# Attention of 896 tokens ahead of a two-layer MoE pair, with each narrowed weight used for two chunks of tokens

## The chip, the cores and the metric

One core of one Trainium2 chip runs the whole program as a single launch. The metric is the device time in microseconds (us). TensorE (PE) multiplies, VectorE (DVE), ScalarE (ACT) and GpSimd (POOL) do elementwise work, and SyncE (SP) issues the DMA transfers.

## What is computed

The reference is a chain of three stages over 2304 tokens (4 batches of 576) with a model width of 512:

```python
scores = scale * q @ k.T + bias            # 8 heads of 64; window of 128 keys, causal
attn = softmax(scores);  x = attn @ v      # -> x: 2304 x 512
h = x @ w_in;  g = relu(h) ** 2            # first MoE, d_ff 2048
x = g @ w_out
P = sinkhorn(softmax(x @ w_gate))          # second MoE: 8 experts of 1024
out = sum_e P[:, e] * (relu(x @ w1[e]) @ w2[e])
```

The weights w_in and w_out arrive as 64-bit floats. The kernel makes 32-bit values out of them by bit operations ("narrowing") and splits each into a high and a low part, so that a product is three matmuls.

## The kernel before, in words

**Chunks.** The first MoE walks over five chunks of tokens (lines 50 to 53), 384, 512, 512, 512 and 384 wide, which the text calls chunk zero to chunk four. In each chunk 16 turns f (loop at line 683) take one slice of 128 hidden units: `gemm1` (line 122) makes the product into the bank h1 with 12 matmuls, lines 695 to 698 apply relu (ACT) and the square (DVE), `split_sb` splits the result into gh and gl (ACT, POOL), and, two turns later (LAG), `moe1_tail` (line 488) adds 12 matmuls into four accumulator banks. After the last turn `moe1_finish` takes the accumulators out and `gate_sums` (line 515) runs eight small matmuls into lt; these mark the end of a chunk in the trace.

**Weights.** In chunk zero `moe1_load` (line 473) calls `fetch` (line 458) for the 64-bit slice (tile u, three buffers, 512 KB), `narrow` (line 434), which is three ACT and five DVE instructions, and stores the result to DRAM (d_in for w_in, d_out for w_out, 512 KB each). Tile a (from w_in) has three buffers and b (from w_out) four. In later chunks a and b are loaded back from DRAM. The loads run one or two turns ahead.

**Attention.** The work is cut into 32 units (line 368): a batch, a pair of heads, and either its first 384 tokens ("early", tiles i = 0, 1, 2) or the rest ("rest", tiles 3 and 4). `attention_load` (line 187) fetches q, k and v of a unit, `attention_qk` (line 205) transposes and splits q and k, `attention_scores` (line 257) handles one tile's scores up to the normalised weights, `attention_weights` (line 302) transposes them and splits them into p, and `attention_values` (line 350) multiplies by v and writes the split result into the x of a chunk. `plan` (line 375) writes these steps into one list by hand; in its first run the score step goes two tiles ahead of the weight step and two units alternate, in its second one tile ahead.

**Order.** Before each chunk's turns, line 675 calls `advance` (line 407) to run the list up to what that chunk needs (`needed`, line 401). So four units (384 tokens) come before chunk zero. `part` (line 652), called three times a turn, then hands out the units of the next chunk evenly over the 16 turns: beside chunk zero run the 8 units (20 tiles) for chunk one, beside chunk one the 20 tiles for chunk two, and so on. Units of the first four (`alone`, line 190) rotate their PSUM tiles through more banks: those of the accumulators and of h1 too (`at_ps`, line 162). All instructions up to line 718 are put in order by the framework's scheduler, which starts from the order of the program text; each engine then works through its own list in order, SP's list of DMA issues too.

**Behind it.** From chunk two on nothing differs in the change; the second MoE (two thirds of the time) follows. The lines named in rows: L440 to L454 narrowing, L466/L471 fetches of weights, L481 stores of narrowed weights, L483 loads of a and b, L118 to L120 matmuls of products, L696/L698 relu and square, L109/L110 the split, L282 scores, L322 transposes of the weights, L336 values, L113/L114 splits out of PSUM.

Of the kernel before, what the change touches and what calls it, by code (L numbers as in the profile page):

```python
# [8 lines left out]
F32 = mybir.dt.float32  # L9
F32R = mybir.dt.float32r  # L10
U32 = mybir.dt.uint32
AF = mybir.ActivationFunctionType
# [17 lines left out]
def attention_moe_moe2(  # L30
# [106 lines left out]
    cv = cvs.enter_context(tc.tile_pool(name="cv", bufs=1))  # L137
    att = ExitStack()
    ap = att.enter_context(tc.tile_pool(name="ap", bufs=1, side="right"))

    rel_i = ap.tile([P, 2 * P], mybir.dt.int32, name="rel_i", tag="kl", bufs=2)
    nc.gpsimd.iota(rel_i, pattern=[[-1, 2 * P]], base=P, channel_multiplier=1)
# [41 lines left out]
                    tbias[j * TAIL : (j + 1) * TAIL, hp, :], bias[0:TAIL, 2 * hp + j, : P + TAIL]  # L184
                )

    def attention_load(b, hp, rest):

        h0 = 2 * hp
        t = {"rest": rest, "alone": b == 0 and not rest}  # L190
        for nm, src in (("k", k), ("q", q), ("v", v)):
            r = t[nm] = ap.tile([P, 3, 2, D], F32, name=f"{nm}raw", tag=f"{nm}raw", bufs=2)
            r0 = 0 if not rest else EARLY - (0 if nm == "q" else P)
            r1 = FULL * P if rest else EARLY
            for j in range(2):
                nc.sync.dma_start(
                    r[:, : (r1 - r0) // P, j, :], src[b, h0 + j, r0:r1, :].rearrange("(t p) d -> p t d", p=P)
                )
            if rest:
                nc.sync.dma_start(  # L200
                    r[:TAIL, (r1 - r0) // P], src[b, h0 : h0 + 2, r1:, :].rearrange("j p d -> p j d")
                )
        return t
# [164 lines left out]
    units = [(b, hp, rest) for b in range(B) for rest in (False, True) for hp in range(NPAIR)]  # L368
    ts = {}

    def load(n):
        if n < len(units):
            ts[n] = attention_load(*units[n])

    def plan():


        out = []

        def run(tiles, first, s_ahead, q_ahead):  # L380
            turned = first
            for j, x in enumerate(tiles):
                while turned <= max(n for n, _ in tiles[: j + q_ahead + 1]):
                    out.append(("q", turned, 0))
                    turned += 1
                out.append(("s", *x))
                if j >= s_ahead:
                    out.append(("t", *tiles[j - s_ahead]))
            out.extend(("t", *x) for x in tiles[-s_ahead:])

        run([(n + j, i) for n in range(0, NPAIR, 2) for i in range(3) for j in range(2)], 0, 2, 1)
        run(
            [(n, i) for n in range(NPAIR, len(units)) for i in (range(3, FULL + 1) if units[n][2] else range(3))],
            NPAIR, 1, 1,
        )
        return out

# [2 lines left out]

    def needed(n):

        b, at = divmod(n - 1, S)
        last = (2 * b + (at >= EARLY) + 1) * NPAIR
        return 1 + max(j for j, x in enumerate(steps) if x[0] == "t" and x[1] < last)

    def advance(n):
        for kind, m, i in steps[done[0] : n]:
            b, hp, rest = units[m]
            if kind == "q":  # L410
                if m == NPAIR:
                    tails_ready()
                attention_qk(m, ts[m])
                ts[m]["p"] = {}
            elif kind == "s":
                attention_scores(hp, ts[m], i)
                if i in (1, FULL):
                    attention_v(m, ts[m])
                    load(m + 2)
            else:  # L420
                attention_weights(ts[m], i)
                attention_values(b, hp, ts[m], i)
        done[0] = max(done[0], n)
# [6 lines left out]
    d_in = [dram.tile([P, 2, DM], F32, name=f"d_in{f}") for f in range(NF1)]  # L430
    d_x2 = [dram.tile([P, NK, HALF], F32, name=f"d_x2{h}") for h in range(2 * NB)]
    d_out = [dram.tile([P, 2, DM], F32, name=f"d_out{f}") for f in range(NF1)]

    def narrow(src, hi, lo):

# [37 lines left out]
    def moe1_load(c, f):  # L473
        out = []
        for j, (nm, dr, nb) in enumerate((("a", d_in[f], 3), ("b", d_out[f], 4))):
            hl = mp.tile([P, 2, DM], F32R, name=nm, tag=nm, bufs=nb)
            if c == 0:
                i = 2 * f + j
                fetch(i + 2)
                narrow(words.pop(i), hl[:, 0], hl[:, 1])  # L480
                nc.sync.dma_start(dr, raw(hl))  # L481
            else:
                nc.sync.dma_start(raw(hl), dr)  # L483
            hl = [hl[:, 0], hl[:, 1]]
            out.append([x.rearrange("p (k f) -> p k f", k=NK) if nm == "a" else x for x in hl])
        return out

    def moe1_tail(c, f, accs, g, b):
        c0, n = chunk(c)
# [177 lines left out]
    for c in range(NCH):  # L667
        c0, n = chunk(c)
        if c == 1:
            cvs.close()  # L670
            xp2 = m1.enter_context(tc.tile_pool(name="xp2", bufs=1))
            for i in range(3, NCH):
                new_x(xp2, i)

        advance(needed(c0 + n))
        if c == NCH - 1:
            att.close()
            p2 = ctx.enter_context(tc.tile_pool(name="p2", bufs=1, side="right"))
            p3s = ExitStack()
            p3 = p3s.enter_context(tc.tile_pool(name="p3a", bufs=1, side="right"))  # L680
            load_q(0)
            for nm, eng in (("b11", 0), ("b21", 1), ("t1", 0), ("t2", 1), ("t3", 0), ("t4", 1), ("b22", 0)):
                x_op(nm, (nc.vector, nc.gpsimd)[eng])
        for f in range(NF1):
            now[:] = c, f
            a, bw = ahead.pop(0)
            todo = c * NF1 + f + (2 if loaded[0] < NF1 - 2 else 1)
            while loaded[0] <= min(todo, len(turns) - 1):
                ahead.append(moe1_load(*turns[loaded[0]]))
                loaded[0] += 1  # L690
            hp, tag = (ps_mm, "mm") if c < NCH - 1 else (ps_at, "at")
            ph = hp.tile([P, 512], F32, name="h1", tag=tag)
            gemm1(ph, a, slice(0, P), c)
            part(1)
            r = rp.tile([P, CH], F32, name="r", tag="r", bufs=2)
            nc.scalar.activation(r[:, :n], ph[:, :n], AF.Relu)  # L696
            g = r
            nc.vector.scalar_tensor_tensor(g[:, :n], ph[:, :n], 0.0, r[:, :n], op0=ALU.max, op1=ALU.mult)  # L698
            gh = rp.tile([P, CH], F32R, name="gh", tag="rh", bufs=3)
            gl = rp.tile([P, CH], F32R, name="gl", tag="rl", bufs=3)  # L700
            split_sb(g[:, :n], gh[:, :n], gl[:, :n])
            if f == 0:
                accs = {}
            gate_logits()
            pending.append((c, f, accs, (gh, gl), bw))
            if len(pending) > LAG:
                t = pending.pop(0)
                moe1_tail(*t)
                if t[1] == NF1 - 1:
                    moe1_finish(t[0], t[2])  # L710
                    gate_sums(t[0])
            part(3)
# [553 lines left out]
```

## Time and profile before

| what | value |
|---|---|
| median of 3 runs | 2176.01 us (2174.59 to 2178.0) |
| profiled execution, span from first to last instruction | 2174.1 us |
| TensorE busy | 2103.4 us, 97% of the span, 11360 matmuls |
| VectorE busy | 1490.4 us, 69% |
| ScalarE, GpSimd busy | 996.3 us (46%), 1070.5 us (49%) |
| DMA | 525.49 MB, 242 GB/s over the span |

Of the profiled execution the span is what was recorded; a whole time of its own beside it is not. The span lies 1.9 us below the median and just below the fastest run. Busy time is a sum over stages with different limits, so the rows further down cut it by stage. A matmul's end is modelled and neighbours overlap, so its busy time is more than what it holds the engine for.

### The profile page before, as it was taken

The page shows a single profiled execution, that of the slowest core. Times are in us where ns is not written, and L with a number is a line of the kernel's source. Part 1 is how long each engine was busy: PE and PEld are TensorE (multiplying, and loading weights), DVE is VectorE, ACT ScalarE, POOL GpSimd, SP SyncE. Part 2 cuts the span into 40 slices and gives each one's busy share as a digit, 9 for nine tenths or more (in the row PEclk, how much of TensorE's full clock was granted, in tenths as well). Part 3 has the DMA queues.
Part 4 walks back from the last instruction along what each step waited for, and adds up shares of the span by engine and source line. Part 5 has one row for each costly group of instructions (what it writes and reads, how often), then busy time and mean ns, then how long its engine had stood idle before and what let it go on. Part 6 is the DMA issues. An engine that isn't in the chain of part 4 may idle for free.

```text
span 2174.1 us, 32629 instructions
## 1 busy us (share of the span) xinstructions
PE 2103.4 (97%) x11360; PEld 1925.0 (89%) x11360; DVE 1490.4 (69%) x2667; ACT 996.3 (46%) x2050; POOL 1070.5 (49%) x709
## 2 busy tenths in 40 slices
PE   6889999999999899999999999999999999999998
PEld 4778777777888788899999899999999999999998
DVE  7998455453244788887788677666778567777666
ACT  6776445443333444444444444444444544444443
POOL 2222223123254777788888544444546445454442
PEclk9899999999999999999999999999999999999999
DMA  6776545445475877687888988777777877778773
GB/s 186 219 246 209 148 148 162 143 148 177 157 259 170 300 276 294 263 331 284 320 287 299 333 275 265 260 260 260 259 260 265 271 260 252 253 258 269 259 260 125
DMA packets 281730, 525.49 MB, mean 242 GB/s; under 512 B 85584, under 2 KB 129760, under 8 KB 277472
## 3 DMA queue, kind: packets, MB, share of 16 engines
q1 hardware_dynamic: 281568, 523.42, 71.5%
q8 instruction: 91, 1.49, 0.3%
q14 instruction: 71, 0.58, 0.1%
HBM read 379.60 MB, written 143.73 MB: 241 GB/s over the span
## 4 chain that ended last, share of the span: by engine, by line
PE 77%; DVE 12%; ACT 3%; DMA 3%; issue 2%; POOL 1%; SPq 1%; ACTq 0%; POOLq 0%; DVEq 0%
PE y L119 9%; PE y L120 9%; PE y L118 9%; PE g L118 9%; PE g L120 9%; PE g L119 9%; PE h L118 3%; PE acc L118 3%; PE h L120 3%; PE h L119 3%; PE xo L336 3%; PE acc L120 3%; PE acc L119 2%; PE sc L282 2%; DVE rl L936 1%
## 5 line engine op out<-in xcount | busy, mean ns | idle before, releaser
L1086 POOL TENSOR_TENSOR rb<-R,rb 128x768 fp32r<-128x768 f32 x95 | 212.3, 2235 | 334.7 <-ACT rb L1081 322.3
L1117 DVE TENSOR_TENSOR a<-y,a 128x384 f32<-128x384 f32 x434 | 240.0, 554 | 180.0 <-PE y L120 178.0
L1086 POOL TENSOR_TENSOR rt<-R,rt 128x768 fp32r<-128x768 f32 x125 | 238.8, 1922 | 146.3 <-issue 61.7
L110 POOL TENSOR_TENSOR gl<-r,gh 128x512 fp32r<-128x512 f32 (+1 forms) x80 | 99.0, 1237 | 355.1 <-ACT gh L109 336.1
L110 POOL TENSOR_TENSOR w2a<-r,w2a 128x1024 fp32r<-128x1024 f32 x64 | 155.2, 2425 | 67.1 <-ACT w2a L109 67.1
L1081 ACT ACTIVATE rt<-R 128x768 fp32r<-128x768 f32 x128 | 107.7, 842 | 148.5 <-DVE R L1068 90.1
L118 PE MATMUL g<-xt,w1o 128*128 128x384 f32 x512 | 173.0, 338 | 0.9 <-ACT u L809 0.6
L120 PE MATMUL g<-xt,w1o 128*128 128x384 f32 x512 | 172.6, 337 | 0.0
L118 PE MATMUL y<-rt,w2o 128*128 128x384 f32 x512 | 172.4, 337 | 0.1
L120 PE MATMUL y<-rt,w2o 128*128 128x384 f32 x512 | 172.5, 337 | 0.0
L119 PE MATMUL g<-xt,w1o 128*128 128x384 f32 x512 | 172.4, 337 | 0.0
L119 PE MATMUL y<-rt,w2o 128*128 128x384 f32 x512 | 172.1, 336 | 0.0
L118 PE MATMUL y<-w2a,rh 128*128 128x512 f32 x384 | 151.1, 394 | 0.0
L119 PE MATMUL y<-w2a,rh 128*128 128x512 f32 x384 | 150.9, 393 | 0.2 <-POOL w2a L110 0.2
L120 PE MATMUL y<-w2a,rl 128*128 128x512 f32 x384 | 150.2, 391 | 0.0
L698 DVE SCALAR_TENSOR_TENSOR r<-h,r 128x512 f32<-128x512 f32 (+1 forms) x80 | 50.9, 636 | 134.5 <-ACT r L696 134.5
L1063 DVE TENSOR_TENSOR R<-R,pb 128x768 f32<-128x768 f32 x128 | 137.8, 1078 | 5.2 <-ACT R L1176 3.0
L118 PE MATMUL y<-rb,w2o 128*128 128x384 f32 x384 | 129.9, 338 | 2.8 <-DVE a L1117 2.1
L119 PE MATMUL y<-rb,w2o 128*128 128x384 f32 x384 | 130.0, 339 | 2.3 <-POOL rb L1086 2.3
L120 PE MATMUL y<-rb,w2o 128*128 128x384 f32 x384 | 129.9, 338 | 0.0
L120 PE MATMUL g<-xb,w1o 128*128 128x384 f32 x384 | 129.2, 336 | 0.0
L118 PE MATMUL g<-xb,w1o 128*128 128x384 f32 x384 | 129.1, 336 | 0.0
(231 smaller groups left out, 6234.4 us busy)
## 6 DMA issues: line engine op xcount, KB each, us to landing
w1o<-d_w SPq DMA_DIRECT2D x448, 256.0 KB, 3.1
w2o<-d_w SPq DMA_DIRECT2D x224, 512.0 KB, 4.0
d_w<-w1a SPq DMA_DIRECT2D x32, 1792.0 KB, 11.7
d_w<-w2a SPq DMA_DIRECT2D x32, 1536.0 KB, 8.1
a<-d_in SPq DMA_DIRECT2D x64, 512.0 KB, 3.8
b<-d_out SPq DMA_DIRECT2D x64, 512.0 KB, 3.6
r<-in_moe_w_dram SPq DMA_DIRECT2D x64, 512.0 KB, 4.3
u<-in_moe_w_in_dram SPq DMA_DIRECT2D x16, 512.0 KB, 4.6
```

The costliest lines, as they stand in the source:

```text
L110: (eng or nc.gpsimd).tensor_sub(lo, src, raw(hi))
L118: nc.tensor.matmul(ps, lhsT=lh, rhs=rh, start=first, stop=False, **kw)
L119: nc.tensor.matmul(ps, lhsT=lh, rhs=rl, start=False, stop=False, **kw)
L120: nc.tensor.matmul(ps, lhsT=ll, rhs=rh, start=False, stop=last, **kw)
L282: nc.tensor.matmul(sc[:, :nk], lhsT=lhs, rhs=rhs, start=x == 0, stop=x == 2)
L336: nc.tensor.matmul(dst, lhsT=l, rhs=r, start=first and n == 0, stop=last and n == 5, skip_group_check=True)
L698: nc.vector.scalar_tensor_tensor(g[:, :n], ph[:, :n], 0.0, r[:, :n], op0=ALU.max, op1=ALU.mult)
L936: nc.vector.scalar_tensor_tensor(rl, src, 0.0, raw(rh), op0=ALU.max, op1=ALU.subtract)
L1063: nc.vector.tensor_mul(r, r, pb[:, None, :].to_broadcast([P, 2, HALF]))
L1081: nc.scalar.activation(x[:, 0], R[m, f, h], AF.Copy)
L1086: eng.tensor_sub(x[:, 1], R[m, f, h], raw(x[:, 0]))
L1117: nc.vector.tensor_add(acc[dst][:, dt], ps[:, :HALF], acc[dst][:, dt])
```

## The change

Attention for 896 tokens instead of 384 is run before chunk zero: the first 12 units instead of 4 are `alone`, and line 675 asks for them. In each turn of chunk zero a second `gemm1` multiplies the same a tile with the x of chunk one, into a bank of the attention's pool; relu and square follow (`squared`), and the result, 128 x 512, is stored to DRAM (d_g, 256 KB a turn). In chunk one a turn has no `gemm1`: `moe1_load` fetches that result in place of a. The calls of `part` in chunk zero then have nothing left to hand out, and those in chunk one hand out chunk two's attention as before. A pool gp of three 128 x 512 tiles is new.

```diff
@@
+    gp = att.enter_context(tc.tile_pool(name="gp", bufs=1, side="right"))
@@
-    def attention_load(b, hp, rest):
+    def attention_load(n):
+        b, hp, rest = units[n]
         h0 = 2 * hp
-        t = {"rest": rest, "alone": b == 0 and not rest}
+        t = {"rest": rest, "alone": n < AHEAD}
@@
+    def units_of(n):
+        b, at = divmod(n - 1, S)
+        return (2 * b + (at >= EARLY) + 1) * NPAIR
+    AHEAD = units_of(starts[1] + widths[1])
@@ def plan():
-        run([(n + j, i) for n in range(0, NPAIR, 2) for i in range(3) for j in range(2)], 0, 2, 1)
+        first = []
+        for n in range(0, AHEAD, 2):
+            if units[n][2]:
+                first.extend((n + j, i) for j in range(2) for i in range(3, FULL + 1))
+            else:
+                first.extend((n + j, i) for i in range(3) for j in range(2))
+        run(first, 0, 2, 1)
         run(
-            [(n, i) for n in range(NPAIR, len(units)) for i in (range(3, FULL + 1) if units[n][2] else range(3))],
-            NPAIR, 1, 1,
+            [(n, i) for n in range(AHEAD, len(units)) for i in (range(3, FULL + 1) if units[n][2] else range(3))],
+            AHEAD, 1, 1,
         )
@@
+    d_g = [dram.tile([P, widths[1]], F32, name=f"d_g{f}") for f in range(NF1)]
@@ def moe1_load(c, f):
+            if c == 1 and nm == "a":
+                g = gp.tile([P, CH], F32, name="g", tag="g", bufs=3)
+                nc.sync.dma_start(g[:, : widths[1]], d_g[f])
+                out.append(g)
+                continue
@@
+    def squared(ph, g, n):
+        nc.scalar.activation(g[:, :n], ph[:, :n], AF.Relu)
+        nc.vector.scalar_tensor_tensor(g[:, :n], ph[:, :n], 0.0, g[:, :n], op0=ALU.max, op1=ALU.mult)
@@
-        advance(needed(c0 + n))
+        advance(needed(starts[1] + widths[1] if c == 0 else c0 + n))
@@
-            ph = hp.tile([P, 512], F32, name="h1", tag=tag)
-            gemm1(ph, a, slice(0, P), c)
-            part(1)
...
+            if c == 1:
+                part(1)
+                g = a
+            else:
+                hp, tag = (ps_mm, "mm") if c < NCH - 1 else (ps_at, "at")
+                ph = hp.tile([P, 512], F32, name="h1", tag=tag)
+                gemm1(ph, a, slice(0, P), c)
+                part(1)
+                g = rp.tile([P, CH], F32, name="r", tag="r", bufs=2)
+                squared(ph, g, n)
+                if c == 0:
+                    ph = ps_at.tile([P, 512], F32, name="h2", tag="at")
+                    gemm1(ph, a, slice(0, P), 1)
+                    keep = gp.tile([P, CH], F32, name="g", tag="g", bufs=3)
+                    squared(ph, keep, widths[1])
+                    nc.sync.dma_start(d_g[f], keep[:, : widths[1]])
```

## Rows read from the trace of the kernel before

**Rows 1.** the page: slices of 54 us (busy tenths), and one costly group

```profile
PE   6889999999999899999999999999999999999998
...
DVE  7998455453244788887788677666778567777666
...
L110 POOL TENSOR_TENSOR gl<-r,gh 128x512 fp32r<-128x512 f32 (+1 forms) x80 | 99.0, 1237 | 355.1 <-ACT gh L109 336.1
```

**Rows 2.** the chain of waits from 0 to 700 us: the gate products closing chunks

```profile
217.41 0.67 PE lt L519 x3
...
362.19 0.69 PE lt L519 x3
...
502.31 0.84 PE lt L519 x3
```

**Rows 3.** windows by stage: length, busy (x count) PE, PEld, DVE, ACT, POOL; clock; DMA

```profile
26.00:62.00 36.00, 32.39 (x177) 26.14 (x177) 30.25 (x118) 25.13 (x81) 4.33 (x6) 0.91 0.47 134
62.00:205.00 143.00, 131.33 (x737) 112.22 (x736) 132.65 (x378) 101.25 (x270) 34.42 (x34) 0.94 0.74 232
...
217.40:362.20 144.80, 142.96 (x754) 110.53 (x754) 68.44 (x241) 66.77 (x195) 33.66 (x36) 0.98 0.50 146
```

**Rows 4.** the chain of waits in 62:205: shares, and two longest pieces

```profile
by line: DMA u<-in_moe_w_out_dram 8.1%; DVE cv L447 7.2%; DVE cv L443 5.8%; PE sc L282 5.7%; PE h L118 5.4%; PE h L119 4.4%; PE h L120 4.3%; DVE cv L451 3.7%; DVE cv L444 3.4%; DVE s L299 3.4%; PE xo L336 3.3%; DVE b L454 3.2%; DVE p L114 3
...
158.82 4.19 DMA u<-in_moe_w_in_dram
164.18 3.95 DMA u<-in_moe_w_out_dram
```

**Rows 5.** windows, all instructions, a stretch with 384-column matmuls alone (columns as rows 3)

```profile
640.00:660.00 20.00, 20.00 (x117) 20.00 (x117) 2.79 (x5) 5.09 (x10) 4.26 (x5) 1.00 0.84 277
```

**Rows 6.** windows of tile h alone: PE, PEld, DVE, ACT busy; clock; DMA of all

```profile
62.00:205.00 143.00, 48.74 (x194) 37.52 (x193) 8.77 (x16) 7.74 (x16) 0.94 0.74 232
...
217.40:362.20 144.80, 51.65 (x192) 35.72 (x192) 11.08 (x16) 9.57 (x16) 0.98 0.50 146
```

**Rows 7.** windows of tile acc alone, columns as rows 6

```profile
217.40:362.20 144.80, 55.69 (x190) 33.12 (x190) 1.88 (x4) 1.64 (x3) 0.98 0.50 146
```

**Rows 8.** groups on VectorE, 26:62: count, busy us, mean ns, idle before

```profile
L114 DVE TENSOR_TENSOR p<-pt,p 128x256 fp32r<-128x256 f32 x20 | 8.3, 417 | 4.5 <-ACT p L113 4.5
...
L296 DVE TENSOR_SCALAR z<-z 128x2 f32<-128x2 f32 x10 | 1.7, 169 | 1.0 <-ACT s L292 0.5
```

**Rows 9.** windows of tile cv (narrowing) alone: DVE, ACT busy; clock; DMA

```profile
62.00:205.00 143.00, 78.46 (x130) 46.89 (x74) 0.94 0.74 232
26.00:62.00 36.00, 6.95 (x12) 5.16 (x8) 0.91 0.47 134
```

**Rows 10.** groups on VectorE, 0:62: narrowing

```profile
L447 DVE SCALAR_TENSOR_TENSOR cv<-u,cv 128x512 uint32<-128x512 uint32 x6 | 4.1, 685 | 0.0
```

**Rows 11.** groups on ScalarE, 62:217

```profile
L440 ACT ACTIVATE cv<-u 128x512 f32<-128x512 f32 x24 | 16.2, 676 | 10.1 <-DVE cv L444 4.4 <-DMA u<-in_moe_w_out_dram 4.3 <-DVE cv L447 0.8
L442 ACT ACTIVATE cv<-u 128x512 uint32<-128x512 uint32 x24 | 16.0, 668 | 0.9 <-DVE cv L451 0.8
...
L453 ACT ACTIVATE a<-cv 128x512 fp32r<-128x512 f32 x13 | 8.2, 629 | 7.1 <-DVE cv L451 7.1
```

**Rows 12.** windows, all instructions (columns as rows 3)

```profile
720.00:740.00 20.00, 18.22 (x85) 16.21 (x84) 14.77 (x24) 7.82 (x13) 14.00 (x11) 0.93 0.96 357
120.00:140.00 20.00, 17.02 (x106) 14.13 (x104) 19.46 (x55) 15.80 (x41) 3.50 (x3) 1.00 0.91 275
40.00:60.00 20.00, 17.36 (x99) 13.86 (x99) 15.64 (x60) 13.76 (x43) 3.08 (x3) 0.83 0.37 111
60.00:80.00 20.00, 17.89 (x87) 14.81 (x87) 17.83 (x52) 13.75 (x39) 4.25 (x7) 0.83 0.61 188
```

**Rows 13.** SP's own waits, 62:205: us in total, times, longest

```profile
SPq L481 <- DVE a L454: 17.6, 12, 3.5
```

**Rows 14.** DMA issues, 217.4:362.2: count, KB each, median us to landing

```profile
a<-d_in SPq DMA_DIRECT2D x16, 512.0 KB, 3.7
```

More of the change, by code (lines that the diff above doesn't have):

```diff
@@ L369, in attention_moe_moe2 @@
     ts = {}
+    def units_of(n):
+        b, at = divmod(n - 1, S)
+        return (2 * b + (at >= EARLY) + 1) * NPAIR
+    AHEAD = units_of(starts[1] + widths[1])
     def load(n):
         if n < len(units):
-            ts[n] = attention_load(*units[n])
+            ts[n] = attention_load(n)
     def plan():
@@ L401, in needed @@
     def needed(n):
-        b, at = divmod(n - 1, S)
-        last = (2 * b + (at >= EARLY) + 1) * NPAIR
+        last = units_of(n)
         return 1 + max(j for j, x in enumerate(steps) if x[0] == "t" and x[1] < last)
@@ L690, in attention_moe_moe2 @@
                 loaded[0] += 1
-            hp, tag = (ps_mm, "mm") if c < NCH - 1 else (ps_at, "at")
-            ph = hp.tile([P, 512], F32, name="h1", tag=tag)
-            gemm1(ph, a, slice(0, P), c)
-            part(1)
[L695 to L698, printed above, removed]
+            if c == 1:
[14 more added lines that the diff above has]
+                    nc.sync.dma_start(d_g[f], keep[:, : widths[1]])
             gh = rp.tile([P, CH], F32R, name="gh", tag="rh", bufs=3)
```

## The prediction, made before the change was run

> **What bounds the kernel now.** I read the page first for the whole, then windows by stage, then the chain of waits and groups of one stage. On the page VectorE is full in the first tenth and TensorE from there on [rows 1]. The windows cut that at the gate products that close a chunk [rows 2]: closing chunk zero at 217.4 us, chunk one at 362.2, chunk two at 502.3; I call these the marks. Three stages differ [rows 3]. From 26 to 62 us attention of 384 tokens runs almost alone: VectorE 30.25 of 36 us. From 62 to 205 us chunk zero, the narrowing of the weights and the attention of chunk one run together: VectorE 132.65 of 143 us. From 217.4 to 362.2 VectorE needs only 68.44 of 144.8 us, and TensorE 142.96. So VectorE sets the first 205 us and TensorE the next 157. The chain in 62:205 agrees: it passes through narrowing instructions and weight fetches, not through TensorE alone [rows 4]. Matmul ends are modelled, so I take prices of TensorE from counts: 117 matmuls of 384 columns in 20 us, 0.171 us each [rows 5]; for 512 columns I estimate 0.171 x 512/384 = 0.228, below the 51.65/192 = 0.269 that their busy time gives [rows 6].
>
> The change doesn't remove arithmetic. It moves 192 matmuls of 512 columns from a TensorE-bound stage into one with VectorE bound, and pays by moving 20 attention tiles (one score/weight step of two heads; 8 of rest units, 12 of early ones) out of that stage to where nothing runs beside them.
>
> **The change, part by part.** Everything behind the mark of chunk one is untouched, so the time changes by as much as that mark moves.
>
> *What leaves chunk one.* Between the marks lie 192 products into h: 14 turns of chunk one and the first 2 of chunk two [rows 6]. 14 x 12 = 168 leave: 168 x 0.228 = 38.3 us at the low price, 45.2 at 0.269. I take 38.3, because the gaps that sit in the higher price belong to the attention beside it and stay. So the new mark of chunk zero may come at 217.4 + 38.3 = 255.7 before anything is lost. The remaining tail products and attention must still fill the engine: 144.8 less 384 x 0.228 (the products into h and acc [rows 6, 7]) less 1.4 for the gate's 8 leaves 56 us for 20 tiles, 2.8 each. With half the matmuls a tile's chain (scores, VectorE maximum, ScalarE exponential, transposes, values) has less cover. Bounds: 0, and 20 x (3.6 - 2.8) = 16 us if a tile then costs the 3.6 us of the lone attention below. VectorE's and ScalarE's 67 us fit easily into 106, so I take 2.
>
> *The front.* From 26 to 62 us ten tiles pass [rows 8] in 36 us, with 6.95 us of VectorE for narrowing among them [rows 9]. A lone tile costs 23.3/10 = 2.3 us if VectorE had no gap, 3.6 if all of the 36 us is its price, 29.05/10 = 2.9 with narrowing alone taken off. I take 2.9, since the idle time in that stretch is ScalarE's and TensorE's reply (VectorE waits 4.5 us for the copies of p [rows 8]) and recurs. The front then ends at 62 + 20 x 2.9 = 120 us; bounds 108 and 134. Also moved: eight more units' loads (6 to 9 small transfers each) go ahead of most fetches of weights on SP. SP is in order; the lone stretch has DMA engines 0.47 busy [rows 3], so they fit. Narrowing during the front stays at about the six weights begun by 62 us [rows 10], as the ring of a has three tiles. Scores, weights and values of these units now also rotate through the accumulator banks and the h bank, so chunk zero's products hardly run ahead: 0.
>
> *Chunk zero.* A turn (one f) holds 12 + 12 matmuls of 384 columns and now 12 of 512: 24 x 0.171 + 12 x 0.228 = 6.8 us of TensorE. VectorE: two narrowings, 78.46/26 = 3.0 us each by their busy time [rows 9], nearer 2.5 without the overlap of neighbours, plus 8.77/16 = 0.55 for the old squares and 11.08/16 = 0.69 for the new [rows 6]: 6.2 to 7.3 us. ScalarE: three copies of 0.63 to 0.68 us per weight [rows 11] and three more of about 0.5 to 0.6 are under 6 us; POOL's 1.24 us [rows 1] has room. DMA: per turn 2 MB as before plus the 256 KB store, 2.36 MB: 6.6 us at the fastest stretch, 357 GB/s with the engines 0.96 busy; 8.6 us at the 275 GB/s of 120:140, where they were 0.91 busy with the small rows of q, k and v in the mix [rows 12]. Those rows leave this stage, so I sit nearer the first. Three resources within 10% of each other never overlap cleanly: I take 7.4 us for the 13 turns whose weights aren't ready, 6.8 for the other 3, and 2 for filling: 13 x 7.4 + 20.4 + 2 = 119 us, where today the turn takes 143/16 = 8.9. Bounds: 111 (all TensorE) and 134 (all at 8.6).
>
> The new store on SP waits for its square; the next fetch and the store of narrowed weights stand behind it. Today SP waits for narrowed a 17.6 us in this stage [rows 13] and three u tiles cover it; a square comes inside the same turn, so nothing. In chunk one 16 loads of 256 KB replace 16 of 512 KB and land in about 3.7 us [rows 14] in a turn of over 6, one turn ahead: nothing.
>
> *Sum.* Before the mark of chunk zero TensorE also does two turns' attention for chunk two, 2.5 tiles x 2.8 = 7 us. Mark: 120 + 119 + 7 = 246, against 255.7: 9.7 earlier, less 2 for thinner cover: 7.7 us. The profiled span of 2174.1 becomes 2166.4. The median of the runs shown, 2176.0, is 1.9 us above that span, so **2168 us**.
>
> **Rivals.** About 0.2% (4.4 us) is what a measurement of this kernel can tell from no change.
>
> *Transfers hold the turn (slower).* Place: lines 466 to 481 in chunk zero. An a tile now lives through two products, so with three tiles the next narrowing, its store and its fetch bunch up. At 8.6 us a turn chunk zero takes 13 x 8.6 + 22.4 = 134 and the mark comes at 261; with the 2 us the kernel is 7 us slower: 2183. It decides from 8.0 us a turn. For it: ScalarE already waits 4.3 us for fetches here [rows 11] and the longest pieces of the chain are fetches [rows 4]. Against: the 0.74 share contains the small rows that leave.
>
> *Nothing measurable.* The front at 3.2 us a tile costs 6 more, or chunk one's cover falls 6 us short: 2174. For it: tiles at 3.6 wall in the only stretch that shows them alone.
>
> *A larger gain.* If the longer front keeps VectorE at the 93% of rows 3 (2.5 us a tile) and chunk zero runs at TensorE's 6.8, the mark comes at 112 + 111 + 7 = 230, and with the 2 us the gain is 24 us, 2152; half of the way there is 2160. Against: three resources would have to mesh.
>
> *The lower clock in the front.* The granted clock averaged 0.83 in 40:60 and in 60:80 [rows 12], a third of the time at 1.2 GHz after TensorE had waited for attention, and 1.00 in 120:140. If the whole added front ran at 1.2 GHz, a tile's TensorE work, (144.8 - 51.65 - 55.69)/20 = 1.9 us [rows 3, 6, 7], would double to 3.8 a tile; the front would end at 138, and the kernel would be 18 us slower than my sum: 2186. The trace speaks against it: the whole lone stretch had 0.91 [rows 3], and VectorE was the one that was full. The Trainium skill, "TensorE: Matmul & The Clock Gate", section on HAM oscillation, says that a TensorE which keeps pausing is throttled again and again to half its rate, which speaks against moving attention to where no matmul fills its pauses; the row agrees only in part, and by that rule the time would be the 2186.
>
> **How the numbers follow.** My forecast (2162 to 2171) 0.39; larger gain 0.18; nothing measurable 0.21; transfers or a front at 3.6 (2179 to 2185) 0.17; clock 0.05. Faster 0.57, same 0.21, slower 0.22. The range leaves out the far end of the larger gain and of the clock: 2157 to 2185.
>
> **What would show it.** The front ends (last score step of attention before the first product of 512 columns into h2) near 120 us; the gate of chunk zero near 246, of chunk one near 354, with about 108 us between. In chunk zero TensorE is full, VectorE about 0.85, and a turn is 7 to 7.5 us. Wrong if a fetch is the main wait there, if the turn is above 8.0, if the front passes 128, or if TensorE waits for ScalarE's or VectorE's copies by over 10 us in chunk one. If the mark of chunk one moved and the end did not by as much, the stages behind it are not as untouched as I say.

## The result, and the profile after

The changed kernel takes **2187.9 us** (median of 8 runs, 2184.5 to 2196.2) against 2177.6 for the kernel before beside it: a ratio of 1.0054, 95% interval 1.0038 to 1.0069. It is slower by half a per cent where I had forecast a gain of 8 us. The profiled execution has a span of 2185.9 us, inside the range of the runs; the one before had 2174.1.

The page's slices (54.6 us each), to be held against [rows 1]:

```profile
PE   6999999999999899999999999999999999999998
...
DVE  7769655453243788888778677667778577777666
...
PEclk9589999999999999999999999999999999999999
```

VectorE stood at nine tenths in the second and third slice; now the fourth alone of the first five has a nine. In the second slice (55 to 109 us) TensorE is busy and its granted clock is 0.5. The rest of this section works out what that digit costs.

The chain of waits shows the gate products that close chunks zero, one and two, answering to [rows 2]:

```profile
258.27 0.53 PE lt L543 x3
...
370.02 0.70 PE lt L543 x3
...
508.46 0.84 PE lt L543 x3
```

Mark one moved from 362.2 to 370.0, 7.8 later. A repeat of the changed kernel (e15) had it 6.1 later. In this pair of profiles 7.8 of the 11.8 us between the spans are thus lost before mark one. Behind it the changed kernel loses 4.0 us more: 1.7 are regained by mark two, 5.7 go later. The repeat's profile gains 0.7 there. I could not tie these pieces to a cause.

Windows of the changed kernel by stage, columns as [rows 3]:

```profile
26.00:62.00 36.00, 32.83 (x167) 25.44 (x167) 28.64 (x124) 24.02 (x79) 2.50 (x4) 0.81 0.43 118
62.00:142.00 80.00, 74.52 (x362) 60.29 (x362) 58.06 (x226) 48.89 (x162) 12.04 (x19) 0.66 0.33 86
69.40:117.20 47.80, 45.78 (x190) 37.20 (x190) 33.09 (x129) 26.34 (x86) 5.17 (x8) 0.50 0.43 113
142.00:249.00 107.00, 107.00 (x553) 98.71 (x553) 84.88 (x149) 64.07 (x118) 19.99 (x17) 1.00 0.81 283
258.00:370.00 112.00, 109.81 (x616) 84.62 (x615) 64.73 (x244) 61.45 (x193) 34.94 (x38) 0.97 0.56 162
```

| stage | forecast | measured | off by |
|---|---|---|---|
| front: 62 us to the end of the moved attention | ends at 120 | ends at 142 | +22 |
| chunk zero and what follows, to mark zero | 126 us (to 246) | 116.3 us (to 258.3) | -9.7 |
| mark zero to mark one | 108.5 us | 111.8 us | +3.3 |

The forecast of the last row is 144.8 - 38.3 + 2. The three make +15.6, which is what mark one missed the forecast by (362.2 - 7.7 = 354.5 forecast, 370.0 measured). So the 20 moved tiles took 80 us, 4.0 each, not 2.9. Chunk zero was better than I thought.

The chain of the changed kernel in 62:142, by line, and three pieces of it, all value matmuls. The first is 17 matmuls of a rest unit's tile, of 64 to 192 columns, inside 69.4 to 117.2, where the granted clock is 0.50. The second is 17 of early units, of 128 and 256 columns, behind it at 1.00. The third is six of 256 columns at 0.50 again:

```profile
by line: PE xo L338 33.6%; PE sc L284 20.4%; PE pt L324 14.8%; PE tp_k L220 3.4%; PE tp L220 2.7%; DMA kraw<-in_k_dram 2.7%; PE tp_q L220 2.5%; DVE p L114 2.4%; ACT p L113 2.3%; DVE xl L114 2.3%; issue 1.7%; ACT s L294 1.6%; PE pt L315 1.4%
...
72.66 3.66 PE xo L338 x17
...
123.79 2.19 PE xo L338 x17
...
136.29 1.28 PE xo L338 x6
```

The end of the front hangs on TensorE, not on VectorE: values, scores and transposes are 69% of the chain. Seventeen value matmuls take 3.66 us at a granted clock of 0.50 (1.2 GHz) and 2.19 at 1.00 (2.4 GHz), although the second seventeen have more columns. Within such a row the number of columns hardly matters: at 0.50 one takes 0.215 us with 64 to 192 columns and 0.213 with 256.

The pace of attention as a whole can be read at both levels in this one kernel:

```profile
117.20:130.80 13.60, 13.12 (x82) 9.86 (x81) 10.96 (x53) 9.65 (x34) 2.01 (x2) 1.00 0.20 45
130.80:137.60 6.80, 6.52 (x28) 5.63 (x28) 4.93 (x22) 3.65 (x13) 0.00 (x0) 0.50 0.00 0
```

At 0.50 (69.4 to 117.2 and 130.8 to 137.6) it did 218 matmuls in 54.6 us, 0.25 us each; at 1.00 (117.2 to 130.8) 82 in 13.6 us, 0.17 each. The repeat has 0.24 (71.9 to 89.0 and 92.4 to 119.7) and 0.16 (119.7 to 133.4). By the kernel's text the 20 moved tiles have 360 matmuls, 18 a tile: 4.5 us at the lower level and 3.0 at the higher. At the higher pace the 218 would have taken 36 us. So I estimate that the clock accounts for some 18 of the 22 us by which the front missed. The two stretches are not the same mix of matmuls.

**Theory.** At 1.2 GHz TensorE's own work sets the tile's time; at 2.4 GHz the 20 tiles would cost about what I forecast. **Rivals:** the order of the tiles, the number of PSUM banks or the replies of VectorE and ScalarE set it, and the clock is a bystander; or the sharing of weights itself does not pay.

### The profile page after: what moved, and what is told of

It is laid out like the page before. It is cut to its first block, busy times and chain, and to the rows that moved or that the text cites. A ratio compares the mean times of both kernels' runs of the same rounds, so it can differ in the third digit from the quotient of the medians.

```text
span 2185.9 us, 32704 instructions
## 1 busy us (share of the span) xinstructions
PE 2120.0 (97%) x11360; PEld 1945.2 (89%) x11360; DVE 1494.4 (68%) x2667; ACT 999.3 (46%) x2050; POOL 1065.4 (49%) x709
## 4 chain that ended last, share of the span: by engine, by line
PE 82%; DVE 8%; ACT 3%; DMA 2%; issue 2%; POOL 2%; SPq 1%; ACTq 0%; POOLq 0%; DVEq 0%
PE y L118 9%; PE y L119 9%; PE y L120 9%; PE g L118 9%; PE g L120 9%; PE g L119 9%; PE xo L338 4%; PE h L118 3%; PE h L120 3%; PE h L119 3%; PE acc L118 3%; PE acc L120 3%; PE acc L119 3%; PE sc L284 2%; PE pt L324 1%
## 5 line engine op out<-in xcount | busy, mean ns | idle before, releaser
L110 POOL TENSOR_TENSOR gl<-r,gh 128x384 fp32r<-128x384 f32 (+1 forms) x64 | 77.4, 1210 | 275.4 <-ACT gh L109 269.7
L120 PE MATMUL g<-xb,w1o 128*128 128x384 f32 x384 | 129.3, 337 | 0.0
L118 PE MATMUL g<-xb,w1o 128*128 128x384 f32 x384 | 129.3, 337 | 0.0
L119 PE MATMUL g<-xb,w1o 128*128 128x384 f32 x384 | 129.0, 336 | 0.0
```

What stands on the lines that cost most here:

```text
L110: (eng or nc.gpsimd).tensor_sub(lo, src, raw(hi))
L118: nc.tensor.matmul(ps, lhsT=lh, rhs=rh, start=first, stop=False, **kw)
L119: nc.tensor.matmul(ps, lhsT=lh, rhs=rl, start=False, stop=False, **kw)
L120: nc.tensor.matmul(ps, lhsT=ll, rhs=rh, start=False, stop=last, **kw)
```

## The experiments

Each is timed against the kernel before on the same chip. A "wide product" is a matmul of 384 columns whose result is overwritten at once.

**Is the sharing or the move at fault?** e3 keeps the attention ahead and takes the shared product away again:

```diff
-            if c == 1 and nm == "a":
+            if False:
...
-            if c == 1:
-                part(1)
-                g = a
+            if False:
+                pass
...
-                if c == 0:
+                if False:
```

> One part alone: attention of 896 tokens goes ahead, but chunk one's first product stays in chunk one, with its weights loaded again; nothing is stored to d_g. Both theories: the front still ends near 142 us at the lower clock. Chunk zero without the second product is then bound by VectorE at 5.5 to 6.5 us a turn, 85 to 105 us, and the 38 us of products go back to chunk one: its closing gate comes near 395 us, the kernel takes 2200 to 2220 us. The difference to the changed kernel (2186) is what the shared weights are worth: I expect 15 to 30 us, so that the forecast's gain existed and the front took it back. If sharing is worth under 5 us, the forecast was wrong there too.

Measured: 2211.3 us (4 runs), ratio 1.0154 (1.0134 to 1.0175). Against the 1.0054 of the change, sharing gives back about 1% (22 us), and moving attention ahead costs 1.5%. The split carries a difference that the edit didn't aim at: e3's front began some 8 us later than the changed kernel's and ends 15 us later.

```profile
62.00:156.90 94.90, 89.27 (x399) 71.63 (x397) 64.29 (x252) 54.49 (x180) 12.48 (x20) 0.62 0.30 77
```

```profile
399.67 0.70 PE lt L543 x3
```

Mark one comes 29.6 us later than in the changed kernel; 15 of them lie in the front, and 15 behind it, where the sharing acts. So the shared product is sound, worth about 15 us by the marks, and the loss is in the front.

**Does wide work raise the clock?** e1, e2 and e7 add one, three and six wide products per head ahead of the scores of the moved units (36, 108 and 216 products; by the 0.171 us of [rows 5], 6.2, 18.5 and 36.9 us). `fill` marks the eight moved units; the number in `range` is 1, 3 or 6:

```diff
-        t = {"rest": rest, "alone": n < AHEAD}
+        t = {"rest": rest, "alone": n < AHEAD, "fill": NPAIR <= n < AHEAD}
...
+        if t["fill"]:
+            for sc in scs:
+                for _ in range(1):
+                    nc.tensor.matmul(
+                        sc[:, :EARLY], lhsT=xh[0][:, 1, :P], rhs=xh[0][:, 0, :EARLY], start=True, stop=True
+                    )
```

> One idle-work matmul (384 columns, real data, overwritten by the first score matmul) per head and score step of the eight units that moved ahead: 36 matmuls, 6.3 us of TensorE at 0.174 us. Theory clock: in the changed kernel TensorE ran at the lower of its two levels from 80.8 to 128.6 us because it paused too often, and that stretched the front from the 120 us forecast to 142; a little more work keeps the level up for part of the front, so the front gets shorter although TensorE has more to do: it ends at 125 to 138 and the kernel takes 2172 to 2184 us. Rival structure: the front is long because of the chain of one tile, its banks and its loads, and the clock only follows; then the added work is hidden or costs up to 12 us (6.3 us at half rate): front ends at 142 to 154, kernel 2186 to 2198.

> Three such matmuls per head: 108 of them, 18.8 us of TensorE at full rate, 37 at half. Theory clock: TensorE stays at its upper level for most of the 62 to 142 us stretch (mean granted clock over 0.85 instead of 0.66), and the front ends near 125 us: 58 us for the 20 tiles plus what of the 18.8 us is not hidden; kernel 2165 to 2178 us. Rival structure: the front grows by 10 to 37 us, kernel 2196 to 2225.

> Six overwritten matmuls of 384 columns per head in the front instead of three: 216, 37.6 us of TensorE at the upper level, 75 at the lower. Theory clock: the level stays up (over 0.95 in 62:142), and the front takes 58 us for the tiles plus most of the added 37.6: it ends at 140 to 158; kernel 2180 to 2202. Rival structure: the front of 142 us grows by the added time that isn't hidden at either level; with 18.8 us hidden completely in the run with three, the next 18.8 are mostly exposed: front past 160, kernel over 2200.

(The low stretch that e1's expectation puts at 80.8 to 128.6 us is the one at 69.4 to 117.2 of the windows.) Measured: e1 2190.4 us, 1.0058 (1.0041 to 1.0075); e2 2186.8, 1.0043 (1.0027 to 1.0059); e7 2196.1, 1.0088 (1.0071 to 1.0105). Windows of e1, e2 and e7 from 62 us to the end of their fronts:

```profile
62.00:147.20 85.20, 80.31 (x415) 63.77 (x414) 60.98 (x234) 50.10 (x168) 12.43 (x19) 0.74 0.31 83
```

```profile
62.00:145.30 83.30, 77.25 (x461) 65.05 (x460) 57.62 (x227) 47.25 (x160) 10.28 (x18) 0.84 0.29 76
```

```profile
62.00:152.30 90.30, 84.66 (x579) 73.39 (x579) 59.51 (x232) 50.29 (x169) 11.05 (x18) 1.00 0.29 74
```

The granted clock rises with the dose, 0.66, 0.74, 0.84, 1.00, but the front does not get shorter. In e7 the reason stands in the chain and in the groups of TensorE in that window: L285, the wide product, is the largest share, while values fall to 286 ns and transposes to 287.

```profile
by line: PE sc L285 28.7%; PE xo L344 17.6%; issue 10.4%; PE sc L290 7.2%; PE pt L330 5.9%; ACT s L300 4.8%; DMA u<-in_moe_w_out_dram 4.4%; DVE p L114 1.8%; DVE xl L114 1.8%; DVE s L307 1.7%; DVE s L293 1.6%; DVE kl L114 1.4%; ACT xh L113 1
...
L344 PE MATMUL xo<-p,vsplit 128*128 128x128 f32 (+3 forms) x168 | 25.7, 286 | 2.8 <-ACT p L113 2.7
L330 PE MATMUL pt<-ident,s 128*128 128x128 f32 x60 | 10.4, 287 | 0.0
```

The same two groups of the changed kernel, in 62:142:

```profile
L338 PE MATMUL xo<-p,vsplit 128*128 128x128 f32 (+3 forms) x161 | 34.2, 366 | 0.1
L324 PE MATMUL pt<-ident,s 128*128 128x128 f32 x57 | 14.2, 376 | 0.4 <-DVE s L301 0.3
```

**Does it matter where they stand?** e9 and e10 put three and six wide products per tile (60 and 120; 10.3 and 20.5 us) into the bank of the transposes, ahead of them; e11 mixes both places (96; 16.4 us). I meant to fill waits for the weights there, but the group of L324 above shows only 0.4 us of idle time before it.

```diff
+        if t["fill"]:
+            for _ in range(3):
+                nc.tensor.matmul(pt[:, :EARLY], lhsT=xh[0][:, 1, :P], rhs=xh[0][:, 0], start=True, stop=True)
```

> The overwritten matmuls move from ahead of the scores into the bank of the transposed weights, ahead of the transposes, where TensorE waits for VectorE: 3 of 384 columns per tile, 60 in all, 10.4 us at the upper level, meant to run in pauses that are there anyway. Theory clock: work in the pauses lifts the level without lengthening the tile; mean clock in 62:142 over 0.8, the front ends between 118 and 135 and the kernel takes 2162 to 2180 us. Rival structure: the level rises too, but the tile stays at 4 us because its banks and its chain hold it: front 140 to 150, kernel 2184 to 2196.

> Six of them per tile, 120 in all, 20.9 us. Theory clock: the level stays at 1.00 from 70 us on; what no longer fits the pauses lengthens the front: it ends between 120 and 140, the kernel takes 2165 to 2185. Rival structure: front over 142 although the level is 1.00, kernel 2186 to 2200.

> Three per tile ahead of the transposes and one per head ahead of the scores: 96 in all, 16.7 us, spread over both places. Theory clock: the level stays over 0.9 in 62:142, front 120 to 138, kernel 2163 to 2183. Rival structure: front over 142, kernel 2186 to 2200.

Measured: e9 2183.6 us, 1.0036 (1.0022 to 1.0050); e10 2186.3, 1.0048 (1.0033 to 1.0063); e11 2184.0, 1.0042 (1.0025 to 1.0060), with ten runs spread over 2176.1 to 2195.7. Windows of e9, e10 and e11 to the end of their fronts:

```profile
62.00:139.00 77.00, 70.92 (x425) 59.22 (x426) 57.87 (x227) 49.10 (x163) 13.41 (x19) 0.87 0.35 91
...
62.00:146.40 84.40, 77.96 (x493) 66.07 (x492) 60.24 (x232) 50.86 (x165) 12.45 (x19) 0.94 0.32 84
...
62.00:151.00 89.00, 83.78 (x482) 68.52 (x482) 63.08 (x244) 52.23 (x172) 12.84 (x17) 0.88 0.30 80
```

At best 3 us of the front come back, and e9's interval overlaps that of the change. In e1 and e10 the time and the front lie in the range that I had given to the rival, in e2, e9 and e11 they fit neither; of these runs in e7 alone the theory's ranges held. Now take each front's length times its granted clock, less the products added at 0.171 us. That is the time its attention would take at 2.4 GHz if TensorE set it:

| kernel | front, us | clock | added, us | at 2.4 GHz, us |
|---|---|---|---|---|
| changed | 80.0 | 0.66 | 0 | 52.8 |
| e1 | 85.2 | 0.74 | 6.2 | 56.9 |
| e2 | 83.3 | 0.84 | 18.5 | 51.5 |
| e7 | 90.3 | 1.00 | 36.9 | 53.4 |
| e9 | 77.0 | 0.87 | 10.3 | 56.7 |
| e10 | 84.4 | 0.94 | 20.5 | 58.8 |
| e3 | 94.9 | 0.62 | 0 | 58.8 |

It lies between 51 and 59 us whatever the clock (e11, whose front began some 8 us later, as e3's did, gives 61.9). That is 2.6 to 2.9 us a tile. It is a conversion, not a measurement: no run had these tiles alone at the higher clock throughout, and VectorE is busy 58.06 us of the changed kernel's front, narrowing included. Together with the 3.0 that the changed kernel's own pace at the higher level gives, it says that my price fits the higher clock only.

That the clock is no bystander shows in e9, in the 27.2 us ahead of 137.2:

```profile
110.00:137.20 27.20, 27.10 (x190) 22.88 (x188) 21.41 (x89) 19.02 (x66) 3.34 (x5) 1.00 0.15 33
```

Of the 190 matmuls 28 are wide products. So at 1.00 a matmul of attention cost 0.17 us with the wide products in its price; at 0.50 the changed kernel needed 0.25 without any.

**Is it the order, or the banks?** e4 lets the two rest units of a pair alternate tile by tile; e8 takes the accumulators' and h1 banks from the moved units.

```diff
-                first.extend((n + j, i) for j in range(2) for i in range(3, FULL + 1))
+                first.extend((n + j, i) for i in range(3, FULL + 1) for j in range(2))
```

```diff
-        t = {"rest": rest, "alone": n < AHEAD}
+        t = {"rest": rest, "alone": n < NPAIR}
```

> The two rest units of a pair alternate tile by tile as the early ones do, instead of one after the other. Rival structure: the tail tiles wait for their own unit's score tile, which the alternation covers, so the front gets 5 to 10 us shorter: 2176 to 2182. Theory clock: the work and the pauses stay about the same, the level too; front within 4 us of 142, kernel 2183 to 2190, unless the denser order lifts the clock in 62:110 (over 0.75 on the mean), which the windows would show.

> Only the mark of the moved units is undone: units 4 to 11 rotate over the attention's own three PSUM banks, not over the accumulators' and h1's too. Rival structure (banks bound the front): the front grows by over 8 us, kernel above 2194, or, if the wider rotation is what blocks, shrinks as much. Theory clock: TensorE at its lower level is the bound, banks matter little: the front within 6 us of 142, at a level of 0.5 to 0.7; since the accumulators are free, chunk zero's first products can run inside the front, which takes up to 12 us off or lifts the level: 2172 to 2192.

Measured: e4 2186.5 us, 1.0039 (1.0025 to 1.0054), front to 142.5 at a clock of 0.64: the order alone does nothing there. e8 2198.1, 1.0109 (1.0094 to 1.0124):

```profile
62.00:164.00 102.00, 87.87 (x433) 70.88 (x433) 61.14 (x228) 52.45 (x165) 14.48 (x20) 0.71 0.26 68
```

The attention ends at about 164 us though the clock is a little higher. Of the 22 us more, the 73 products of chunk zero that ran among the tiles (37 into h, 36 into acc) account for 12.5; TensorE, busy 0.93 of the changed kernel's front, is busy 0.86 here. The theory of the clock alone had no room for the other 10 us nor for a kernel 12 us slower than the change: banks count once there are only three.

**Less of TensorE's work, none added.** In e14 the moved units do only the first of the three passes in scores and values; their low-order passes are left out.

```diff
...
-        for x in range(3):
+        passes = 1 if t["fill"] else 3
+        for x in range(passes):
...
-            for l, r in ((lh, rh), (lh, rl), (ll, rh)):
+            for l, r in ((lh, rh), (lh, rl), (ll, rh))[: 1 if t["fill"] else 3]:
...
```

> The eight moved units (4 to 11) do only the first of the three passes in scores and values; the low-order passes of those units are left out, nothing else. Per tile of two heads that takes 4 of 6 score matmuls and 8 of 12 value matmuls away. Theory (at the lower clock TensorE's own work sets a tile's time, front 80 us for 20 tiles): the front from 62 us ends at least 20 us earlier, at 110 to 122 instead of 141.9, the granted clock over it stays at 0.5 to 0.75, gate zero comes 18 to 30 us earlier than in the changed kernel, and the time falls from 2188 to 2160 to 2172. Rival (the order of the work, VectorE's and ScalarE's replies or the number of banks set the tile's time, and the clock is only a bystander): the front ends less than 8 us earlier, at 134 or later, and the time stays at 2181 or above.

Measured: 2172.9 us, 0.9988 (0.9976 to 1.0000). The front ends at 126.5:

```profile
62.00:126.50 64.50, 53.12 (x205) 37.31 (x205) 51.52 (x219) 45.05 (x155) 11.05 (x18) 0.60 0.33 82
...
L339 PE MATMUL xo<-p,vsplit 128*128 128x128 f32 (+3 forms) x65 | 17.3, 386 | 4.9 <-ACT p L113 4.9
```

It is 15.4 us shorter at a clock that stays low (0.60), between the 20 of my theory and the 8 of its rival, and nearer the first. Without 46% of the attention's matmuls (196 are left besides 9 products of chunk zero, from 361) the front is 19% shorter. So TensorE's work at the lower clock does set the tile's time, but only until some 15 us are gone: then TensorE waits for p, and VectorE (51.52 of 64.5) stands close behind.

**Is the front better beside chunk zero?** e5 and e6 give chunk one's attention to the first 4 and 8 turns of chunk zero, as in the kernel before, and share the weights from then on.

```diff
-    AHEAD = units_of(starts[1] + widths[1])
+    AHEAD = NPAIR
+    SHARE = 4
...
-            if c == 1:
+            if c == 1 and f >= SHARE:
...
-                if c == 0:
+                if c == 0 and f >= SHARE:
```

> Attention for chunk one goes back beside chunk zero, but only beside its first 4 turns, and the shared second product starts at turn 4: 12 turns share, 4 load their weights again in chunk one as in the kernel before. Theory clock: useful wide products (4 turns x 24 of 384 columns) between the attention steps keep the level up most of the time, so turns 0 to 3 with the 20 tiles take about 75 us instead of the 80 us that the tiles alone took; then 12 turns x 6.9 = 83: gate of chunk zero near 227, of chunk one 112 + 11 us later, near 350: kernel 2163 to 2172. If the level stays near 0.66 in 62:142, the tiles keep their 4 us and the kernel takes 2178 to 2190. Rival structure: the tiles take 4 us each whatever runs beside them, plus 4 turns' narrowing: 62 to 150 us or later, kernel 2176 or more at a clock above 0.85.

> The same with 8 turns beside the attention and 8 shared. Both theories: the mix is nearer to the kernel before, whose clock averaged 0.94 there; VectorE has 8 x 5.9 + 48 = 95 us of work, so the 8 turns take about 100 us; 8 x 6.9 = 55 more; gate of chunk zero near 222, of chunk one near 358: kernel 2168 to 2176. Theory clock says the mean level in 62:160 lies between that of the 4-turn version and 1.

Measured: e5 2183.0 us, 1.0034 (1.0021 to 1.0047); e6 2186.6, 1.0052 (1.0037 to 1.0067). With products beside the attention the clock is higher, in e5 0.87 until the attention ends at 171:

```profile
62.00:171.00 109.00, 99.53 (x536) 81.03 (x536) 88.07 (x294) 69.55 (x208) 22.12 (x25) 0.87 0.49 144
```

The scheduler let more than the 4 turns into this stretch: 173 products of chunk zero start in it, 167 of 384 columns and 6 of 512, 29.9 us by their prices. Less these, 4.0 us a tile are left, with three banks: no cheaper than in the changed kernel, though the clock is higher. This is what I had written down for the rival, so the clock alone does not make a tile cheap. With less sharing less is saved, too.

**Wide work that has to be done anyway.** The value products of the early units ahead of chunk zero go to an accumulator bank for one half of the head pairs and to the bank of h1 for the other, so chunk zero's first products hardly begin before the front is through. e12 takes the h1 bank out of that rotation; e13 adds two wide products per tile as well (40; 6.8 us).

```diff
-    xo_early = [(ps_mm, "mm"), (ps_acc, "acc")]
+    xo_early = [(ps_acc, "acc"), (ps_acc, "acc")]
```

> In the changed kernel the value products of the early units rotate over the accumulator banks and the h1 bank; here over the accumulator banks alone, so that chunk zero's first products into h1 (384 columns, work that has to be done anyway) may run between the tiles. Theory (wide products lift the level, and useful ones cost nothing): products into h1 and h2 appear before 140 us, the mean clock of the front rises from 0.66 to 0.70 or more, the front ends within 4 us of 141.9, gate zero comes 4 to 8 us earlier, and the time is 2179 to 2184. Rival (fewer banks cost more than the lifted level gives): front past 146, gate zero no earlier, 2187 or more.

> The edit of e12 together with two overwritten products of 384 columns ahead of the weight transposes of each moved tile (40 products, 7 us). Theory: the mean clock of the front is 0.8 to 0.9; at about 52 us of full-rate work plus 7 it ends at 130 to 138 with chunk zero's first products (up to 6 us) done; gate zero 8 to 14 us earlier than in the changed kernel, time 2174 to 2181, level with the kernel before at best. Rival (added products cost what the level gives, and banks count): 2184 to 2190.

Measured: e12 2175.3 us, 0.9992 (0.9980 to 1.0004); e13 2177.7, 1.0023 (1.0004 to 1.0042). Of e12 there is no trace to read. This chip was another one than that of the first runs, so the changed kernel (e15), e12's kernel (e16) and the kernel before with the same one-line edit (e17) went to one chip together:

> The changed kernel as it is, on the same chip as the two next runs, since the last three runs lay lower against the kernel before than those ahead of them and were on another chip. If the chip makes the difference, it comes at 0.998 to 1.002 of the kernel before; if the edits did, at 1.004 to 1.007 as the first time.

> The kernel of e12 again (value products of the early units off the h1 bank), since that run left no usable profile. Theory: it repeats 0.998 to 1.002 of the kernel before and comes 8 to 14 us below the changed kernel on the same chip; its profile shows products into h1 between the tiles before 140 us, a mean clock from 62 us to the front's end of 0.75 or more, and gate zero 8 us or more earlier. If the products into h1 merely run ahead, with no effect on the clock, gate zero comes at most 6.3 us earlier (36 products of 0.171 us) and the clock stays under 0.7.

> The kernel before with the same edit (its first four units' value products off the h1 bank). If the edit helps any kernel that begins with attention alone, the kernel before falls by 2 us or more too; theory: in the kernel before chunk zero's weights are not narrowed in time to run ahead of 62 us by more than a turn, so it stays within 3 us of it.

Measured: e15 2190.0 us, 1.0061 (1.0040 to 1.0082): the chip makes no difference. e16 2173.9, 0.9988 (0.9973 to 1.0002): the edit takes 16 us off the changed kernel and brings it level with the kernel before. e17 2181.7, 1.0019 (1.0002 to 1.0036): it does not help the kernel before, and more likely harms it (I had said within 3 us; it is 5 slower).

Windows of e16, and of its tile h alone, from 62 us to the end of its front; and its chunk zero:

```profile
62.00:138.00 76.00, 70.09 (x391) 57.81 (x391) 60.80 (x227) 49.82 (x166) 14.68 (x21) 0.78 0.34 90
...
62.00:138.00 76.00, 11.00 (x31) 7.93 (x32) 1.66 (x3) 1.45 (x3) 0.78 0.34 90
...
142.00:249.00 107.00, 104.52 (x542) 94.42 (x540) 90.06 (x161) 63.53 (x124) 16.94 (x16) 1.00 0.87 299
```

Thirty-one products of chunk zero run between the tiles (six more ran before 62 us), and the mean clock is 0.78 instead of 0.66. The front ends 4 us earlier although it holds 31 x 0.171 = 5.3 us more work: 76 x 0.78 - 5.3 = 54 at 2.4 GHz, in line with the table. Marks zero and one in its chain of waits come 8.5 and 9.7 us earlier than in the changed kernel:

```profile
249.76 0.52 PE lt L543 x3
...
360.32 0.70 PE lt L543 x3
```

Measured from the repeat e15, they come 9.3 and 8.0 us earlier. Had the products only run ahead, the gain would have stopped at 6.3 (38 products of 384 columns, two of them into acc, and one of 512, less two of 512 that ran ahead in the changed kernel too); so the clock seems to have a part in it. That part can't be cleanly split from the bank's own.

e18, the last, adds e4's order to e16:

> The kernel of e16 with the tiles of the two rest units of a pair alternating, as in e4. In e4 that brought 1.4 us beside the changed kernel at most. Theory (TensorE's work at the granted clock is the bound, the order is not): 0.997 to 1.000 of the kernel before, the front ending within 3 us of 138 and chunk one's gate within 3 us of 360. Rival (the order of the tiles still costs once the clock is up): the front ends before 134, and the kernel is at 0.996 or lower, ahead of both.

Measured: 2179.7 us, 1.0008 (0.9991 to 1.0025), level with the kernel before; mark one at 359.0. Nothing that I ran beats the kernel before by more than can be measured.

## Why the prediction was wrong

**The step that failed is the front's price**, "62 + 20 x 2.9 = 120 us". It took a duration from 26:62, where the granted clock was 0.91 [rows 3], and carried it to a stretch where it was 0.66. The 2.9 was about right for 2.4 GHz (2.6 to 2.9 by the conversion in seven kernels, 3.0 by the changed kernel's own pace there), and the front measured 4.0 a tile. I had the mechanism as a rival, with its price ("the front would end at 138", 2186 us), and gave it 0.05. Front (142) and time (2188) came near that, in part by luck: the rival had the whole front at 1.2 GHz at 3.8 us a tile, where 54.6 of 80 us were, at a pace of 4.5.

**Why I gave it so little.** I argued that "VectorE was the one that was full" and that the lone stretch had 0.91. Both were true of ten tiles that came with narrowing. But [rows 12] had the warning: 0.83 in 40:60 and in 60:80, where TensorE was busy 17.4 and 17.9 of 20 us. I read 0.83 as the cost of pauses that would not grow. (Whether products of chunk zero run beside the tiles does not settle it either: 51 start in 60:80 at 0.83, and 51 in 120:140 at 1.00.) The changed kernel shows that the level stays down with few pauses: in 69.4:117.2 TensorE is busy 45.78 of 47.80 us and the clock is 0.50 throughout.

The Trainium skill, "TensorE: Matmul & The Clock Gate", section on HAM oscillation, puts the low clock down to waits in which TensorE pauses. The trace agrees for the fall at 69.4: in 59.1:69.4, ahead of it, TensorE was busy 8.09 of 10.30 us.

```profile
59.10:69.40 10.30, 8.09 (x55) 6.13 (x53) 9.08 (x29) 7.93 (x25) 3.44 (x6) 1.00 0.38 98
```

For the 47.8 us that follow the section gives no reason, nor for the next fall, at 130.8, which came after 13.6 us with TensorE busy for 13.12; there the measurement goes beyond it, and why the level stays down is open.

**Chunk zero, "13 x 7.4 + 20.4 + 2 = 119"**, was 12 us too dear: 107 us, TensorE busy for all of it, 6.7 us a turn. (What follows it, to mark zero, took 9 instead of 7.) "Three resources within 10% of each other never overlap cleanly" was wrong here. VectorE had 84.88 of 107 (0.79, forecast 0.85) and the DMA engines 0.81. Tile cv (narrowing) and tile h (products) of the changed kernel in that window, answering to [rows 9] and [rows 6]:

```profile
142.00:249.00 107.00, 67.48 (x115) 41.14 (x67) 1.00 0.81 283
...
142.00:249.00 107.00, 79.31 (x382) 68.61 (x382) 19.81 (x32) 17.20 (x32) 1.00 0.81 283
```

The rival that transfers hold the turn fell with it, though fetches of weights now land in 5.4 and 4.7 us and ScalarE waits for them 7.3 us in all. Seven weights were narrowed before chunk zero (forecast about six), and the 0 for "chunk zero's products hardly run ahead" was right, and e16 shows what that 0 cost.

```profile
L455 ACT ACTIVATE cv<-u 128x512 f32<-128x512 f32 x21 | 14.1, 669 | 8.5 <-DMA u<-in_moe_w_in_dram 4.4 <-DMA u<-in_moe_w_out_dram 2.9 <-DVE r L510 1.1
...
u<-in_moe_w_in_dram SPq DMA_DIRECT2D x10, 512.0 KB, 5.4
u<-in_moe_w_out_dram SPq DMA_DIRECT2D x10, 512.0 KB, 4.7
d_g<-g SPq DMA_DIRECT2D x16, 256.0 KB, 2.9
```

**Chunk one.** The marks lie 111.8 us apart, not 108.5: "thinner cover" was 2 in my sum and came out at 5.3, inside its bounds of 0 to 16. **Behind mark one** I had "untouched"; in profiled pairs the end moved by 4 (the first) and less than 1 us (e15) otherwise than mark one did. The medians (10.3 and 13.5 us) lie further apart than the marks (7.8 and 6.1) in both, and that remainder stays open.

## What to carry to other kernels

A duration of a TensorE-heavy step holds for the granted clock of the stretch that it was read in. Before a phase of narrow matmuls is moved to where it runs alone, price it at both levels, and give the lower one weight wherever the profile has the same work alone at a clock below 1. Here work beside it that was needed anyway (37 products more ahead of the front's end, 6.3 us) brought the marks 8.0 to 9.7 us forward, and a PSUM bank in the wrong rotation was what kept it out; overwritten wide products raised the clock too, but cost most or all of what they gave.

## What was unexpected of the hardware

A TensorE that is busy does not by that keep its higher clock: 47.8 us at 1.2 GHz with 45.78 us busy, on the narrow matmuls of attention (128 to 256 columns for a score, 64 to 256 for values). Ends of matmuls are modelled, so short pauses may hide in that figure. With wide products among them the mean rose step by step (0.74 with 36, 0.84 with 108), and with 216 it was 1.00. e9 with 60 had 0.87 and e2 with 108 had 0.84, so how many there are does not settle it alone; e16, with 31 products that had to be done anyway, had 0.78.
